# Threshold attention and a multiplicative feed-forward: scheduler-chosen order against a fixed slot order, with token-major P·V, stacked tails and paced weight loads

## Chip, cores, metric

One core of one Trainium2 chip. The metric is device time in microseconds (us) of that core; a lower time is better. Runs of one kernel spread by 1 to 3% here, so times are medians and comparisons are ratios with a 95% interval. A ratio is the mean time of one kernel's fast runs over the mean of the other's fast runs of the same rounds, so it is not quite the ratio of the medians that are quoted. The experiments ran on several chips, each beside the kernel before on the same one.

## The reference

```
scores = q @ k.T / 8                          # 8 batches x 8 heads, 576 x 576, head_dim 64
keep   = scores >= max(scores, -1) - tau
attn   = softmax(where(keep, scores, -1e9))
x      = heads_merged(attn @ v)               # 4608 tokens x 512
out    = ((x @ w1) * (x @ w2)) @ w3 @ w_out   # 512 -> 1024 -> 1024 -> 512
```

The inputs are float32. The kernel splits q and k into a bf16 high part and a bf16 low part and stacks them to a contraction of 128, so that scores are nearly exact; `w3 @ w_out` is multiplied once on the chip ("the merge"). It works on pairs of heads: 32 pairs, each with 9 units of 128 query rows (two heads x 4 blocks of 512 rows, and one unit for the two 64-row tails).

## The kernel before

The program is written as a loop over units, but without a fixed order: the scheduler chooses each engine's order by priorities. The parts that matter here (cuts marked with `...`):

```
# transposes of q and k: 64-row tails of two heads, and 4 blocks of 128 rows for each head
for hh in range(2):
    nc.tensor.transpose(tp[:, M + hh*R : M + (hh+1)*R], h[nm + "hlt"][:, h0 + hh, :, :], ident[0:64, 0:64])
    for j in range(4):
        nc.tensor.transpose(tp[:, c0:c0 + 128], hl[:, hh, j, :, :], ident[:, :])
...
PATH = "PAPAPAPAA"                       # which of two ways each unit takes
# A: copy scores to sc with their maximum (VectorE); Prelu, then Exp with row sums (ScalarE)
# P: maximum only (VectorE); e = Exp(S) (ScalarE); pm = (S >= thr) * e with row sums (VectorE): S stays in PSUM
...
# P.V, feature-major: 64 rows for each head, 512 tokens wide; the reciprocal row sums are split into bf16
# parts, transposed and spread over 128 rows by "selector" matmuls (bm, tl), copied by ScalarE, multiplied in
nc.tensor.matmul(av[o, :], lhsT=vb[:, hh, g, :], rhs=pT[:, :, g + 5*hh, :], start=(g == 0), stop=(g == 4))
...
# weights: 9 loads with a cast on the GpSimd DMA queue, issued in the first dozen units; then the merge
# at the end: feed-forward of the tail rows of batches 0-6 (448 rows), of the last batch, of the last tail
```

The softmax here doesn't subtract the row's maximum and nothing guards it: scores larger than these inputs give would overflow.

## Time and profile before

| | before |
|---|---|
| median of the first 3 runs | 653.55 us (648.12 to 661.48) |
| median in the rounds with the changed kernel | 650.84 us |
| profiled run, span | 654.1 us |
| mean granted TensorE clock | 0.927 |

Engines: PE is TensorE's matmuls, PEld its weight loads, DVE VectorE, ACT ScalarE, POOL GpSimd. These are the page's totals (busy us, share of the span, instructions) and its slices of the span in 40 parts (busy tenths; PEclk is the granted clock, DMA the mean busy share of the 16 DMA engines):

```profile
PE 536.2 (82%) x3790; PEld 286.1 (44%) x3848; DVE 444.1 (68%) x1277; ACT 390.2 (60%) x798; POOL 209.3 (32%) x463
PE   2502679789798989898998998998899998898995
PEclk9855689989999899978999999998899999998996
DMA  7999999887879678966988678977786567553101
```

PE's 82% overcounts, because the ends of pipelined matmuls overlap. PE does little in the first tenth of the span (2, 5, 0 and 2 tenths busy), where the DMA row is full. At the end DMA falls away and PE works on.

The windows of the same run (the stretch and its length, busy us and instructions of PE, PEld, DVE, ACT and POOL, then clock, DMA share and GB/s):

```profile
0.00:50.00 50.00, 12.69 (x84) 7.32 (x85) 13.60 (x46) 9.97 (x18) 27.62 (x59) 0.79 0.99 197
50.00:100.00 50.00, 29.38 (x166) 14.49 (x167) 20.37 (x61) 18.53 (x37) 11.80 (x26) 0.69 1.15 164
600.00:654.10 54.10, 46.86 (x251) 21.52 (x251) 11.72 (x24) 15.61 (x32) 0.00 (x0) 0.90 0.14 40
```

One piece of its chain of waits (start, us, what ended last):

```profile
25.50 45.50 DMA pT<-pm x2
```

In the first 100 us PE has 42 us of busy time; the chain stands 45 us on the attention's DMA transposes (pT from pm) while weights load. In the last 54 us PE runs almost alone.

The waits (engine, line, what it waited for: us in total, times, longest):

```profile
PE S L186 <- DVE pm L233: 35.3, 21, 23.7
PE S L186 <- DMA kB<-kT: 18.7, 9, 8.7
```

PE waits for score tiles in PSUM that the mask (pm) still reads, and for the copy kB of k with its halves exchanged.

### The profile page before, as it was taken

What the parts mean: (1) busy time and instruction counts of PE and PEld (TensorE: products, weight loads), DVE (VectorE), ACT (ScalarE), POOL (GpSimd) and SP (SyncE); (2) the same over time, 40 slices, a digit from 0 to 9 for tenths busy, and PEclk for the clock granted to TensorE, in tenths of its full rate; (3) what the DMA queues carried; (4) which work ended last, traced back from release to release, by engine and by line L of the source; (5) the groups of instructions that cost most, each with busy time, mean ns of one, the idle gap of its engine ahead of it and who ended that gap; (6) DMA issues with size and microseconds to landing.
All of it is one profiled execution on the core that took longest, in us unless ns stands there. A gap on an engine that the chain in (4) does not pass through costs nothing.

```text
span 654.1 us, 11488 instructions
## 1 busy us (share of the span) xinstructions
PE 536.2 (82%) x3790; PEld 286.1 (44%) x3848; DVE 444.1 (68%) x1277; ACT 390.2 (60%) x798; POOL 209.3 (32%) x463
## 2 busy tenths in 40 slices
PE   2502679789798989898998998998899998898995
PEld 1301335445354555444454454544444554453443
DVE  1602447888778787878888887885779887982221
ACT  0501356866577667856676767675667667773332
POOL 6643114442334243424343434341523331000000
PEclk9855689989999899978999999998899999998996
DMA  7999999887879678966988678977786567553101
GB/s 196 222 178 133 154 202 209 162 182 130 162 129 226 145 165 146 228 134 125 180 172 215 146 166 167 211 111 156 189 171 134 100 140 128 96 91 108 40 17 73
DMA packets 232315, 98.80 MB, mean 151 GB/s; under 512 B 198976, under 2 KB 224576, under 8 KB 231232
## 3 DMA queue, kind: packets, MB, share of 16 engines
q1 hardware_dynamic: 229040, 92.83, 70.6%
q0 software_dynamic: 3216, 5.24, 4.9%
q8 instruction: 30, 0.49, 0.4%
q14 instruction: 29, 0.24, 0.1%
HBM read 39.32 MB, written 9.44 MB: 75 GB/s over the span
## 4 chain that ended last, share of the span: by engine, by line
PE 53%; DMA 17%; DVE 13%; ACT 8%; issue 5%; POOL 2%; SPq 1%; DVEq 0%; POOLq 0%; ACTq 0%
PE ab L302 15%; PE S L186 10%; DMA pT<-pm 8%; PE yp L318 8%; PE av L281 6%; PE tp L162 5%; DMA kB<-kT 5%; DVE pm L233 3%; DVE sc L219 3%; DVE junk L229 3%; ACT y L224 3%; DMA w3t<-w_324 2%; PE tp L158 2%; PE wp L101 2%; PE tl L291 2%
## 5 line engine op out<-in xcount | busy, mean ns | idle before, releaser
L186 PE MATMUL S<-kT,qT 128*128 128x288 bf16 x512 | 140.3, 294 | 45.7 <-DVE pm L233 35.3
L224 ACT ACTIVATE y<-sc,thm 128x576 bf16<-128x576 f32 x160 | 122.8, 770 | 61.6 <-DVE thm L223 61.1
L186 PE MATMUL S<-kB,qT 128*128 128x288 bf16 x512 | 138.8, 295 | 19.0 <-DMA kB<-kT 18.7
L186 PEld LDWEIGHTS <-qT 128*128 128x128 bf16 x1024 | 94.5, 100 | 119.0 <-DMA kB<-kT 45.2
L233 DVE SCALAR_TENSOR_TENSOR pm<-S,thr,e 128x576 bf16<-128x576 f32 x128 | 103.7, 810 | 41.5 <-DMA pT<-pm 31.7
L219 DVE TENSOR_SCALAR_CACHE_REDUCE sc<-S 128x576 f32<-128x576 f32 x160 | 118.9, 748 | 15.2 <-PE S L186 11.5
L229 DVE TENSOR_SCALAR_CACHE_REDUCE junk<-S 128x576 bf16<-128x576 f32 x128 | 95.5, 746 | 31.7 <-PE S L186 31.1
L232 ACT ACTIVATE e<-S 128x576 f32<-128x576 f32 x128 | 81.9, 641 | 43.7 <-DVE junk L229 43.3
L226 ACT ACTIVATE pm<-y 128x576 bf16<-128x576 bf16 x128 | 86.9, 679 | 22.8 <-DMA pT<-pm 21.1
L307 ACT ACTIVATE ah<-ab 128x512 bf16<-128x512 f32 (+2 forms) x80 | 44.2, 553 | 75.3 <-PE ab L302 74.6
L310 DVE TENSOR_TENSOR ab<-ah,ab 128x512 bf16<-128x512 bf16 (+2 forms) x80 | 50.6, 632 | 49.1 <-PE ab L302 46.7
L318 PE MATMUL yp<-wcb,ab 128*128 128x512 bf16 (+1 forms) x276 | 72.4, 387 | 1.1 <-issue 0.2
L302 PE MATMUL ab<-xm,w2b 128*128 128x512 bf16 x245 | 67.9, 389 | 0.9 <-issue 0.2
L302 PE MATMUL ab<-xm,w1b 128*128 128x512 bf16 x232 | 66.6, 390 | 2.1 <-issue 1.5
L252 POOL CAST rhl<-rcp 128x9 bf16<-128x9 f32 x32 | 6.2, 194 | 183.8 <-DVE rcp L250 162.6
L150 POOL CAST khl<-kf 128x256 bf16<-128x256 f32 x64 | 24.0, 396 | 68.3 <-PE tp L162 68.2
L302 PEld LDWEIGHTS <-w2b 128*128 128x128 bf16 x320 | 29.5, 100 | 30.0 <-issue 9.7
L151 POOL TENSOR_TENSOR qhl<-qf,qhl 128x256 bf16<-128x256 f32 x64 | 41.9, 668 | 0.9
L151 POOL TENSOR_TENSOR khl<-kf,khl 128x256 bf16<-128x256 f32 x64 | 41.8, 667 | 0.6
L322 ACT ACTIVATE ys<-yp 128x512 f32<-128x512 f32 (+1 forms) x37 | 21.9, 592 | 31.3 <-PE yp L318 31.1
L302 PEld LDWEIGHTS <-w1b 128*128 128x128 bf16 x320 | 28.4, 101 | 27.2 <-issue 4.8
L281 PE MATMUL av<-pT,vb 128*64 128x512 bf16 x256 | 37.5, 416 | 2.6 <-DMA pT<-pm 2.0
(78 smaller groups left out, 743.7 us busy)
## 6 DMA issues: line engine op xcount, KB each, us to landing
kB<-kT SPq DMA_DIRECT2D x64, 144.0 KB, 2.9
kf<-in_k_dram SPq DMA_DIRECT2D x16, 512.0 KB, 4.5
qf<-in_q_dram SPq DMA_DIRECT2D x16, 512.0 KB, 5.2
vf<-in_v_dram SPq DMA_DIRECT2D x16, 512.0 KB, 4.4
out_dram<-ys SPq DMA_DIRECT2D x8, 1024.0 KB, 4.8
pT<-pm SPq DMA_TRANSPOSE x128, 3.5
w_324<-in_moe_w_dram POOLq DMA_DIRECT2D x4, 512.0 KB, 15.7
kt<-in_k_dram SPq DMA_DIRECT2D x16, 64.0 KB, 2.8
```

The lines of the kernel that those rows point to most:

```text
L151: nc.gpsimd.tensor_tensor(hl[:, hh, :, 1, :], src, hl[:, hh, :, 0, :], ALU.subtract)
L186: nc.tensor.matmul(sp[:, half, 0:HB], lhsT=t["qT"][:, q0:q0 + 128], rhs=kk[w][:, c0:c0 + HB], start=(w == 0), stop=(w == 1))
L219: nc.vector.tensor_scalar(sc[:, :].rearrange("p (a b) -> p a b", a=2), sp, 1.0, -3e38, ALU.mult, ALU.max, accum_out=thr[:, :])
L224: nc.scalar.activation(y[:, :], sc[:, :], AF.Prelu, scale=-1.0, bias=thm[:, :], alpha=0.125 / CUT)
L226: nc.scalar.activation(dst, y[:, :], AF.Exp, scale=-CUT, accum_out=rs)
L229: nc.vector.tensor_scalar(junk[:, :, :], sp, margin, -3e38, ALU.subtract, ALU.max, accum_out=thr[:, :])
L232: nc.scalar.activation(e[:, :, :], sp, AF.Exp, scale=0.125)
L233: nc.vector.scalar_tensor_tensor(out=dst.rearrange("p (a b) -> p a b", a=2), in0=sp, scalar=thr[:, :], in1=e[:, :, :], op0=ALU.is_ge, op1= ...
L281: nc.tensor.matmul(av[o, :], lhsT=lhsT, rhs=rhs, start=(g == 0), stop=(g == 4))
L302: nc.tensor.matmul(p[:, 0:nt], lhsT=w[:, c, f * 128:(f + 1) * 128], rhs=x(c), start=(c == 0), stop=(c == 3))
L310: nc.vector.tensor_tensor(ab[:, 0:nt], ah[:, 0:nt], ps[1][:, 0:nt], ALU.mult)
L318: nc.tensor.matmul(yp[0:c1 - c0, :], lhsT=abs_[f][:, c0:c1], rhs=wcb[:, f, :], start=(f == 0), stop=(f == NF - 1))
```

## The change

Its intent: every engine gets a fixed order in slots, one 128-row query unit a slot, with loads, casts, transposes, P·V and feed-forward placed by hand into slots; P·V becomes token-major with a column of ones in V, which gives the row sums; tails of two heads are stacked to 128 rows; weights come in 20 loads, one every second slot. The core of the diff (cuts marked):

```
-    PATH = "PAPAPAPAA"
+    PATH = "AAPAAPAAP"
+    def maximum(n, u):                     # all units: copy to SBUF with maximum, so PSUM is free at once
+        nc.vector.tensor_scalar(sc..., sp[:, :, 0:HB], 1.0, -3e38, ALU.mult, ALU.max, accum_out=mx[:, :])
+        nc.gpsimd.tensor_scalar(thr[:, :], mx[:, :], margin, None, ALU.subtract)     # was on VectorE
+    def mask(n, u): ...                    # one slot later: Prelu, Exp or (sc >= thr) * e, no accum_out
...
-            tp[:, M + hh * R:M + (hh + 1) * R] <- two 64-row transposes
+            src = hl[:, i, :, :] if i < 4 else hlt[:, hp, :, :] if i == 4 else hl[:, i - 1, :, :]
+            nc.tensor.transpose(tp[:, i * 128:(i + 1) * 128], src, ident[:, :])      # 9 of 128 rows
...
+        for un in range(10):               # P.V: 128 tokens x (64 + ones column), 5 contractions each
+            for g in range(5):
+                nc.tensor.matmul(dst, lhsT=lhsT, rhs=rhs, start=(g == 0), stop=(g == 4))   # 65 columns
+        nc.vector.reciprocal(rcp, a5[:, :, :, D])
+        nc.vector.tensor_tensor(x..., a5[:, :, :, 0:D], rcp..., ALU.mult)
+        # x is transposed back by PE and copied to xm and xt by ScalarE
-        rcp, rhl (GpSimd), rT, rTs, bm, tl, bc: the selector matmuls and their copies
...
+    with tc.manual_schedule():
+        for t in range(total + U9):
+            scores(n, u); maximum(unit t-1); evacuations; mask(unit t-2); exponent(unit t-1)
+            # casts, loads, transposes of later pairs in set slots
+            if t < 48:
+                if t % 2 == 1: next(weights, None)      # 20 loads of 512 KB
+                if t >= 30:    next(merging, None)      # the merge, slots 30 to 47
+            # P.V of the pair before in slots 4 to 7; one feed-forward step in the other slots
+            # tail rows fed forward as batches 0-3, 4-6, 7 (before: 0-6, 7)
```

## The prediction

> **What bounds it now.** No engine is full: the page shows PE 82% (pipelined, overcounted), DVE 68%, ACT 60%, POOL 32%. Three stretches count:
> - Start: in the windows, PE is busy 12.7 and 29.4 of the first two 50 us, while the DMA share is 0.99 and 1.15. The chain of waits has 45.5 us on the pT transposes from 25.5 us on: weight loads swamp the DMA engines. The attended blocks xm of the first two pairs end at 77 and 106 us.
> - Steady: from 116.5 to 584.2 us the timeline shows 28 pairs, 16.7 us each.
> - End: the last xm is at 595.5, and 58.5 us of feed-forward (FFN) follow, on PE almost alone.
>
> **Steady limit.** From starts of neighbouring matmuls in the timeline: 288 columns 123 ns, 512 columns 216 ns, 128-column transposes 56 ns. A pair's scores cost 4.6 us, transposes 1.0, FFN 24x216 = 5.2. P*V and row sums take about 2.2, the 64-row transposes about 0.7 more than full ones (132 and 151 ns around them against 56). So PE needs 13.5 of 16.7 us; the rest is waits (S waits for DVE pm 35 us and for kB 19 us in all).
>
> **What changes, per pair.**
> - PE: 50 matmuls of 65 columns replace the 10 wide ones, the selector matmuls and their transpose. The one-batch tail already has 64-column matmuls with fresh 128-column weights every 28 to 29 ns: estimate 50x30 = 1.5 us, plus 0.3 for transposing back. Stacked tails drop the drains. The Trainium skill ("TensorEngine Tiling (Array Packing)", Key Properties) says changing the tiling mode drains the engine; the 132/151 ns agree. Sum about 12.8 us, near 13.3 at the steady clock (about 0.96).
> - DVE: the copying maximum for all units, 9x0.70; three masks instead of four, from SBUF, 3x0.70; two copies 1.5; normalization 1.1; FFN 1.4: about 12.4 us. Thresholds go to POOL.
> - ACT: six two-pass units instead of five, but no 0.19 us accumulator reads: about 11.3 us. POOL about 7.
> - DMA hardly changes: 2.85 MB a pair, about 10.3 us of engine time at uncontended packet times (18 ns for 256 B).
>
> Summing each slot's larger load gives 15.6 us a pair; perfect elasticity gives 13.4. I take 14.5 (1.61 us a slot).
>
> **Sum.** First scores at about 12 us, 288 slots x 1.61 = 464; early congestion: the weights' 32 us of DMA time now spread over 40 slots beside 45 us of attention traffic, costing about 20 rather than 54; the end 36 (drain 8, last batch 96x216 = 21, small tail and store 7), because seven batches' tails move inside. Total 532 us. All on the critical path: start about 40, end about 25 (partly paid back inside), steady about 65.
>
> Predicted 532 us, 80% range 498 to 572; faster by over 2%: 0.95, within 2%: 0.03, slower: 0.02.
>
> **What would show it.** Windows: PE busy above 40 of 50 us from about 100 us on. Pair spacing about 14.5 us. Waits: no 45 us wait on pT; after the last scores about 36 us. P*V matmuls about 30 ns apart. The half-clock windows between 29 and 77 us mostly gone (skill, "TensorE: Matmul & The Clock Gate", Part 1: an idle window halves the clock; the trace's 0.5 records around the idle stretches agree).
>
> **What would make it wrong.** Fixed order turns one late transpose or threshold (POOL behind a 1.3 us subtraction) into a stall of all engines: 16 us a pair, 580. P*V at 60 ns a matmul: +45 us. Start still DMA-bound: +20. Better elasticity: 500.

## The result

| | before | changed |
|---|---|---|
| median | 650.84 us | 592.67 us (586.59 to 595.14) |
| ratio of fast runs | 1 | 0.9109 (0.8997 to 0.9222) |
| profiled span | 654.1 us | 593.4 us |

The direction was right, the size was not: 592.67 us lies 21 us above the upper end of the stated range.

A yardstick used all through: the start of the first maximum operation of each head pair on VectorE (every ninth of these 288 operations). It cuts a run into four stretches. The prediction's terms, put into the same stretches (12; five pairs of 14.5 and 20 of congestion; 26 pairs of 14.5; a last pair of 14.5 and an end of 36), add up to its 532.

| stretch (profiled runs) | before | predicted | changed | changed minus predicted |
|---|---|---|---|---|
| start to first maximum | 17.8 | 12.0 | 11.2 | -0.8 |
| pairs 0 to 4 | 120.3 | 92.5 | 117.6 | +25.1 |
| pairs 5 to 30, 26 of them | 437.9 (16.85 each) | 377.0 (14.5 each) | 399.4 (15.36 each) | +22.4 |
| pair 31 and the end | 78.1 | 50.5 | 65.2 | +14.7 |
| sum | 654.1 | 532.0 | 593.4 | +61.4 |

The page of the changed kernel, the same four lines:

```profile
PE 484.5 (82%) x4683; PEld 319.8 (54%) x4744; DVE 412.6 (70%) x923; ACT 411.3 (69%) x682; POOL 241.1 (41%) x542
PE   4447507699898789878987999998998999998895
PEclk9777857889999899989999999998999999999996
DMA  5999997996769978796979596989599978555102
```

PE still has the weak start with a full DMA row under it: only the very first slices are better than before. The windows say the same, and the last line is the stretch from the last maximum on:

```profile
0.00:50.00 50.00, 25.46 (x194) 17.62 (x195) 23.16 (x52) 21.86 (x33) 27.84 (x70) 0.78 0.95 208
50.00:100.00 50.00, 23.05 (x229) 15.97 (x230) 22.13 (x50) 21.05 (x33) 22.13 (x43) 0.71 1.07 160
550.00:593.40 43.40, 35.19 (x210) 17.22 (x213) 9.21 (x21) 12.22 (x28) 0.00 (x0) 0.89 0.11 38
```

PE was twice as busy as before in the first 50 us, and less busy in the second 50. The waits of the changed kernel that answer to those shown before:

```profile
ACT y L278 <- POOL thr L243: 38.8, 42, 8.8
PE wp L118 <- DMA w3t<-w_815: 23.9, 3, 20.3
PE S L218 <- DVE sc L240: 15.1, 19, 5.6
PE av L307 <- DMA pT<-pm: 12.7, 6, 3.9
PE av L307 <- DMA pTm<-pms_74: 8.2, 7, 2.6
```

The wait of S for the mask is gone and the one for kB nearly so (1.4 us). New, or grown from about 2 us each, are PE's waits at the merge (wp, for the DMA-transposed w3t) and at P·V (av).

**The PE part of the prediction held, as far as the trace shows it.** Taking the starts of neighbouring matmuls in the trace, and counting for each at most its columns at 2.4 GHz plus 3 ns (about the formula of the Trainium skill, "TensorE: Matmul & The Clock Gate", Back-to-back issue gap; the spacings in this trace agree, see the last section), PE's work is 12.6 to 12.8 us in three steady pairs of four and 9.5 us in the fourth, which has less feed-forward (10 to 12 matmuls of it against 26 to 28); the prediction said 12.8 on average, this is 11.9. The same count gives 11.9 us a pair for the kernel before too (pairs 8 to 19): it leaves out drains and waits, so it cannot show what the change saved on PE. Neighbouring P·V matmuls start 33 ns apart on average (median 32; predicted 30). Nothing there explains 60 us.

### The profile page after: what moved, and what is told of

Read it like the earlier page. It is cut to its first block, busy times and chain, and to the rows that moved or that the text cites. A ratio compares the mean times of both kernels' runs of the same rounds, so it can differ in the third digit from the quotient of the medians.

```text
span 593.4 us, 12945 instructions
## 1 busy us (share of the span) xinstructions
PE 484.5 (82%) x4683; PEld 319.8 (54%) x4744; DVE 412.6 (70%) x923; ACT 411.3 (69%) x682; POOL 241.1 (41%) x542
## 4 chain that ended last, share of the span: by engine, by line
PE 32%; ACT 20%; DMA 18%; DVE 13%; POOL 9%; issue 6%; SPq 2%; DVEq 0%; POOLq 0%; ACTq 0%
PE ab L360 12%; ACT y L278 8%; PE yp L375 7%; DMA pT<-pm 6%; ACT pm L280 6%; PE S L218 5%; DVE sc L240 4%; DMA pTm<-pms_74 4%; POOL khl L154 4%; POOL thr L243 2%; DMA w3t<-w_815 2%; ACT e L269 2%; DVE pm L283 2%; PE tp L191 2%; DVE ab L352 2%
## 5 line engine op out<-in xcount | busy, mean ns | idle before, releaser
L240 DVE TENSOR_SCALAR_CACHE_REDUCE sc<-S 128x576 f32<-128x576 f32 x288 | 211.5, 750 | 45.5 <-PE S L218 35.8
L243 POOL TENSOR_SCALAR thr<-mx 128x1 f32<-128x1 f32 x288 | 74.2, 258 | 284.4 <-DVE sc L240 264.6
L278 ACT ACTIVATE y<-sc,thr 128x576 bf16<-128x576 f32 x192 | 147.5, 768 | 40.3 <-POOL thr L243 38.8
L218 PE MATMUL S<-kT,qT 128*128 128x288 bf16 x512 | 143.5, 299 | 16.3 <-DVE sc L240 15.1
L280 ACT ACTIVATE pm<-y 128x576 bf16<-128x576 bf16 x192 | 131.1, 683 | 16.5 <-DMA pT<-pm 10.6
L352 DVE TENSOR_TENSOR ab<-ah,ab 128x512 bf16<-128x512 bf16 (+3 forms) x88 | 51.8, 588 | 45.1 <-PE ab L360 39.2
L283 DVE SCALAR_TENSOR_TENSOR pm<-sc,thr,e 128x576 bf16<-128x576 f32 x64 | 56.3, 880 | 36.0 <-POOL thr L243 14.4
L349 ACT ACTIVATE ah<-ab 128x512 bf16<-128x512 f32 (+3 forms) x88 | 45.1, 512 | 37.8 <-PE ab L360 37.1
L269 ACT ACTIVATE e<-sc 128x576 f32<-128x576 f32 x96 | 64.0, 667 | 0.0
L307 PEld LDWEIGHTS <-pT 128*128 128x128 bf16 x1280 | 50.3, 99 | 20.2 <-DMA pT<-pm 13.5
L360 PEld LDWEIGHTS <-w2b 128*128 128x128 bf16 x352 | 32.2, 99 | 34.3 <-issue 16.4
L118 PE MATMUL wp<-wo,w3t 128*128 128x512 bf16 x59 | 18.2, 420 | 27.1 <-DMA w3t<-w_815 23.9
L154 POOL TENSOR_TENSOR qhl<-qf,qhl 128x512 bf16<-128x512 f32 x32 | 37.0, 1157 | 8.0 <-DMA qt<-in_q_dram 5.3
```

The source lines that it names most:

```text
L154: lo.tensor_tensor(hl[1], src, hl[0], ALU.subtract)
L218: nc.tensor.matmul(sp[:, half, 0:HB], lhsT=t["qT"][:, q0:q0 + 128], rhs=kk[w][:, c0:c0 + HB], start=(w == 0), stop=(w == 1))
L240: nc.vector.tensor_scalar(sc[:, :].rearrange("p (a b) -> p a b", a=2), sp[:, :, 0:HB], 1.0, -3e38, ALU.mult, ALU.max, accum_out=mx[:, :])
L243: nc.gpsimd.tensor_scalar(thr[:, :], mx[:, :], margin, None, ALU.subtract)
L269: nc.scalar.activation(e[:, :], sc[:, :], AF.Exp, scale=0.125)
L278: nc.scalar.activation(y[:, :], sc[:, :], AF.Prelu, scale=-1.0, bias=thr[:, :], alpha=0.125 / CUT)
```

## The experiments

Each experiment has a label (e1 and so on), by which the text calls it. Starts of pairs come from single profiled runs; n is a pair's number, so that n%4 = 0 to 3 are the four pairs of a batch. The unchanged start of the kernel gave pair 5 at 128.8, 131.9 (e3) and 134.4 us (control, a slow run), so differences under about 5 us in that number are not used.

### 1. No weight bytes (e1, wrong result)

```
-            nc.gpsimd.dma_start(dst, src.rearrange("(c p) f -> p c f", p=128))
+            nc.vector.memset(dst, 0.01)
```

> Wrong result on purpose: each weight load becomes a VectorE memset of the same tile, so the attention part is unchanged but no weight bytes are moved. Theory A (the first five pairs take 117.6 us instead of five times 14.8 because the weight loads share the DMA engines with the transposes): the first maximum of pair 5 comes at 85 to 95 us instead of 128.8, total about 555. Theory B (the fixed order makes every engine wait behind the merge's matmuls, which stand at slots 30 to 47 whether or not their transposed weights have landed): the merge still stands there and still transposes by DMA, so much of the loss stays, pair 5 at 105 us or later, total 570 or more.

Measured: 565.87 us, ratio 0.8659 (0.86 to 0.8717). Pair 5 began at 103.0 us instead of 128.8, so the weights' traffic costs about 26 us. (The 20 memsets are 18 us of new VectorE work, so this may be too small.) That is between the two expectations. Pairs 3 and 4, in which the merge stands, still took 21.1 and 20.2 us against 14.8 in the steady state: 11.7 us that no weight load can explain. The merge is 64 matmuls of 512 columns, at 216 ns each 13.8 us of PE (an estimate from the spacing in the trace). **The prediction's sum has no term for it.** But it is not shown that PE's work is what it costs here: no feed-forward runs beside it before the end of pair 4 (its first matmul starts at 127.3 us in the changed kernel, 101.4 here), and PE waits for the transposed weights in these two pairs, in this run and in the changed kernel (23.9 us, above):

```profile
PE wp L118 <- DMA w3t<-w: 8.0, 3, 5.1
```

The windows of this run:

```profile
0.00:50.00 50.00, 28.54 (x230) 19.28 (x231) 35.16 (x72) 26.86 (x40) 27.98 (x71) 0.86 0.80 188
50.00:100.00 50.00, 35.42 (x354) 22.62 (x354) 38.17 (x78) 29.68 (x48) 20.52 (x41) 0.86 0.80 162
```

The DMA share falls from 1.07 to 0.80 in the second 50 us and PE has 35 us of work instead of 23.

### 2. The merge later (e2)

```
             if t < 48:
                 if t % 2 == 1:
                     next(weights, None)
-                if t >= 30:
-                    next(merging, None)
+            if 45 <= t < 63:
+                next(merging, None)
```

> Right result. Loads unchanged; the merge's steps move from slots 30 to 47 to slots 45 to 62. Theory B: the 24 us in which PE waits for w3t go, total about 570. Theory A: the wait for w3t goes, but the DMA engines have the same bytes to move in the same slots and pT waits take its place, total 583 to 593.

Measured: 595.16 us, ratio 0.9091. Pair 5 began at 106.8 us, 22 us earlier, and then pairs 5 and 6 took 29.4 and 21.4 us instead of 16.5 and 15.1: the gain was given back within two pairs. Theory B's forecast failed: the total did not fall. But this does not show that the 24 us wait for w3t cost nothing in its place, because the edit moves the merge beside the feed-forward. PE's work in pairs 5 and 6, counted as above, is 20.3 and 19.9 us here, against 14.7 and 12.6, and PE waits only 4.8 us for w3t. A part went as theory A has it: in pairs 0 to 4 PE waits 23.6 us for pT and pTm, against 11.8. By these counts the merge was paid as waiting in its old place and as PE work in the new one.

### 3. The tails split otherwise (e3)

```
-                    if n // NP in (4, B - 1):
-                        background.append(ffn_tail(*((0, 4) if n // NP == 4 else (4, B - 1))))
+                    if n // NP in (4, B - 2):
+                        background.append(ffn_tail(*((0, 4) if n // NP == 4 else (4, B - 2))))
-        background.append(ffn_tail(B - 1, B))
+        background.append(ffn_tail(B - 2, B))
```

> Right result. Tail rows are fed forward as batches 0-3, 4-5, 6-7 instead of 0-3, 4-6, 7. If the end is long because the tail of batches 4-6 falls after the last scores (541 to 558 us), which I had put inside the main phase, then about 12 to 15 us go: the end from the last maximum (52.9 us) shrinks to about 40, total about 579. Rival (the drain is limited by the last pair's transposes and P*V, not by that tail): less than 4 us.

Measured: 595.65 us, ratio 0.9096: nothing. The end from the last maximum shrank from 52.8 to 50.0 us only. Feed-forward steps are taken in order, so the tail of batches 4 and 5, now inside, pushed the feed-forward of batch 6 out into the end: its matmuls run on to 562 us in this trace. My reason (a piece of work in the wrong place) was wrong in this form. The end is a backlog of feed-forward steps; it shrinks only if steps are gained elsewhere.

### 4. P·V one slot later (e4)

```
-                if u == 4: att = attend(n - 1)
-                if u in (4, 5, 6, 7): next(att)
+                if u == 5: att = attend(n - 1)
+                if u in (5, 6, 7, 8): next(att)
     # feed-forward steps in all slots but 5 and 6 instead of 4 and 5; a batch's feed-forward starts a slot later
```

> Right result. P*V of a pair one slot later (5 to 8 instead of 4 to 7). If the 19 to 20 us pairs come from PE standing still at P*V for the pTm transpose, these fall to about 16 and the waits of av for pT and pTm (26 us) fall below 12: total about 580. Rival (the DMA engines are behind in those pairs, and whoever asks next waits): waits move to another place, total 588 to 595.

Measured: 613.16 us, ratio 0.9392: 3% slower. The waits of av for transposes did fall away, yet the slow pair stayed at 18.8 us and the others lengthened (pairs 8 to 19: 15.2, 18.8, 16.4, 14.4 for n%4 = 0 to 3, against 12.9, 19.5, 15.1, 14.8). In its window from 205 to 500 us there is a new wait:

```profile
PE xq L322 <- DVE x L314: 26.3, 18, 2.3
```

The normalization x now shares its slot with a mask on VectorE. The expectation failed, and the edit moved two things at once, so it says little about DMA. It does show how tight a hand-placed order is: this shift by one slot cost 20 us.

### 5. Thresholds back on VectorE (e5)

```
-        nc.gpsimd.tensor_scalar(thr[:, :], mx[:, :], margin, None, ALU.subtract)
+        nc.vector.tensor_scalar(thr[:, :], mx[:, :], margin, None, ALU.subtract)
```

> Right result. The threshold subtraction goes from GpSimd back to VectorE, as in the kernel before. If VectorE paces the steady state (a pair without feed-forward takes 12.87 us, one with it 14.8 to 15.1, which is about its extra VectorE work), nine ops of 0.15 us a pair add 1.0 to 1.3 us a pair: total about 620 to 630. Rival: the pace is set by ScalarE waiting for thresholds that GpSimd gives late behind its casts (38.8 us of such waits in all): total 575 to 585.

Measured: 586.26 us, ratio 0.9005 (0.8951 to 0.9058). So VectorE's throughput does not pace the steady state, though it was up to 46 or 47 us busy of 50. The four pairs n%4 = 0 to 3 took 14.8, 15.9, 15.5 and 14.9 us: the fast pair slowed and the slow pair became fast, and the sum hardly moved (61.1 against 62.2). That made me ask what fixes the sum.

### 6. No tail loads (e6, wrong result)

```
-            if hp == 1 and b + 1 < B and u in (2, 5, 8):
+            if False:            # and batch 0's casts are used again
```

> Wrong result on purpose: tail rows are loaded and cast for batch 0 only. If the tail loads, which stand in every pair n%4 = 1 right behind the pTm transpose, make that pair take 19.4 us, it falls to about 16 and the total to about 570. Rival (the backlog in the DMA engines comes from the pair before it, which has the loads of three half blocks and the 1 MB store while it runs at 12.9 us without feed-forward): the pair stays above 18 us, total above 583.

Measured: 588.06 us, ratio 0.8959 (0.8901 to 0.9016), a gain of about 1.6% by ratio whose interval overlaps that of the change. The slow pair fell from 19.5 to 17.9 us only (its profile fell in a slow run). The tail loads have a part in it, but not the main one.

### 7. The half loads in odd pairs (e8)

```
-            if n % 2 == 0 and n + 4 < NPAIR and u in (4, 6, 8):
+            if n % 2 == 1 and n + 3 < NPAIR and u in (0, 3, 6):
```

> Right result. The three 512 KB loads of a half go from even pairs (slots 4, 6, 8) to odd pairs (slots 0, 3, 6), so they leave the fast pair n%4 = 0, which also has the 1 MB store. If the DMA backlog of that pair makes the stall of the next one, pair n%4 = 1 falls from 19.4 to 16 to 17 us: total 575 to 582. Rival (the pair that starts a feed-forward is slow by its own program order): unchanged, 588 to 596.

Measured: 604.36 us, ratio 0.9277: slower. The slow pair fell to 17.4 us, as the DMA theory wants, but pair n%4 = 3 rose from 14.8 to 16.8. The stall moves with the loads; the sum of four pairs stays (62.5 us, pairs 8 to 19), but the pairs after them lengthen too. The profile is of a slow run.

### 8. Scheduler-chosen order (e7)

```
-    with tc.manual_schedule():
+    if True:
```

> Right result. The same instructions, but their order on each engine chosen by the scheduler's priorities as in the kernel before, instead of fixed as written. If the fixed order made the gain: about 630 to 660. Rival (the changed operations made it, and the order cost as much as it gave): 580 to 600.

Measured: 586.25 us, ratio 0.9002 (0.8943 to 0.9061). **With the same instructions and the scheduler's order the kernel is as fast, if not a little faster.** The gain over the kernel before does not come from the order being fixed. (The source order, which gives the priorities, is still the new one.) The slow pairs are there too: 12.7, 17.8, 15.7, 15.4 us (means of pairs 8 to 19, as above). The costliest new wait:

```profile
ACT y L278 <- POOL thr L243: 102.3, 90, 11.4
```

### 9. No half loads from the third half on (e10, wrong result)

```
-                run(load_main(n // 2 + 2, "kqv"[(u - 4) // 2]))
+                halves[n // 2 + 2, nm] = halves[n // 2, nm]      # nm = "kqv"[(u - 4) // 2]
```

> Wrong result on purpose: from the third half batch on, the 512 KB loads of q, k and v are left out and the first two halves are used again; all else is as in the changed kernel. In seven variants so far four pairs take 61 to 65 us together, however the stall is moved. If that sum is set by the DMA engines (share 0.87 to 0.94 there), it falls to 57 to 58 (12.9 + 3 x 14.8), pair n%4 = 1 from 19.4 to about 15, and with the start also relieved the total to 550 to 565. Rival (the sum is set by PE, VectorE and ScalarE in their fixed order, and the stall only makes up for the pair that ran ahead): the sum stays within 1.5 us of 62, total 582 to 592.

Measured: 567.38 us, ratio 0.8686 (0.8639 to 0.8734). The first five pairs took 103.8 us instead of 117.6, and the pairs from 5 on 14.83 us each instead of 15.36. Four neighbouring pairs (from pair 8 on), first in the changed kernel, then in this one; the last two numbers are DMA share and GB/s:

```profile
175.20:188.10 12.90, 11.27 (x133) 7.98 (x133) 11.03 (x27) 10.79 (x18) 6.19 (x13) 1.00 0.80 179
188.10:208.00 19.90, 15.71 (x144) 9.79 (x144) 13.70 (x32) 13.73 (x23) 6.89 (x17) 0.91 1.01 201
208.00:223.10 15.10, 13.60 (x142) 9.06 (x142) 13.32 (x30) 12.28 (x21) 9.26 (x20) 1.00 0.72 164
223.10:237.90 14.80, 13.77 (x145) 9.33 (x145) 11.71 (x28) 12.37 (x21) 6.39 (x14) 1.00 0.79 170
```

```profile
161.20:174.10 12.90, 11.41 (x134) 7.99 (x132) 11.03 (x27) 10.77 (x18) 6.19 (x13) 1.00 0.81 178
174.10:189.60 15.50, 14.10 (x148) 9.09 (x146) 13.73 (x33) 13.72 (x23) 7.00 (x17) 1.00 0.67 150
189.60:204.70 15.10, 13.70 (x144) 9.06 (x141) 13.32 (x31) 12.28 (x22) 9.16 (x20) 1.00 0.59 123
204.70:219.80 15.10, 13.84 (x146) 9.13 (x144) 12.59 (x28) 12.47 (x22) 6.30 (x14) 1.00 0.61 107
```

The second line of each is the slow pair. VectorE and ScalarE do the same work in it (13.7 us busy each), and PE has the same matmuls; what differs is the DMA share, 1.01 against 0.67, and 4.4 us. PE's clock differs too, 0.91 against 1.00, so a part of the 4.4 us (PE is busy for 15.7 us against 14.1) may be the lower clock that came with the waits. In the changed kernel PE stands at P·V in that pair, in the timeline (start, us, instruction, idle before and what ended it):

```profile
197.50 0.30 PE L307 MATMUL av<-vb_78,pT 128*128 128x65 bf16 x4 [1.00 <-DMA pT<-pm]
...
200.60 0.30 PE L307 MATMUL av<-vb_78,pTm 128*128 128x65 bf16 x4 [2.62 <-DMA pTm<-pms_74]
```

The pTm transpose took 4.5 us from issue to landing for that pair, against 2.7 us in an unhurried one. So the DMA engines are behind, and PE is the one that waits, because P·V comes next in its order (in the scheduler's order of e7 too, where P·V waits 18.5 us for transposes in all). This settles a part of the steady miss: 0.53 us a pair, 13.8 us over 26 pairs, and another 13.8 us in pairs 0 to 4. Taking loads away is no version to use; it says what they cost.

### 10. The score tile freed early, in the kernel before (e11)

```
-            nc.vector.tensor_scalar(junk[:, :, :], sp, margin, -3e38, ALU.subtract, ALU.max, accum_out=thr[:, :])
+            nc.vector.tensor_scalar(sc, sp, 1.0, -3e38, ALU.mult, ALU.max, accum_out=thr[:, :])
+            nc.vector.tensor_scalar(thm[:, :], thr[:, :], margin, None, ALU.subtract)
-            exp and mask read sp, thr
+            exp and mask read sc, thm      # and a fourth buffer for sc
```

> One part of the change alone, put into the kernel before: in the exp-and-mask path the maximum op also copies the scores to SBUF, and exp and mask read the copy, so that the PSUM tile of scores is free after the maximum instead of after the mask (one threshold op of 0.15 us more for each such unit). If PE's 35 us of waits for those tiles were a main part of what the steady state gained, 650 falls to 620 to 635. Rival (the gain is in the P*V rewrite and the stacked tails): 645 to 660.

Measured: 662.13 us, ratio 1.0149 (1.0098 to 1.02): 1.5% slower. The wait that this edit removes is replaced by another:

```profile
PE S L186 <- DMA kB<-kT: 46.2, 10, 33.8
```

The 35 us of waits for DVE pm, the largest of PE's in the page before, brought no gain on balance (the edit also adds 128 threshold operations of 0.15 us to VectorE): 23.7 of them are a single wait, during the weight loads of the start, and here PE waits there for DMA instead.

### 11. Scheduler order and thresholds on VectorE (e12: e5 and e7 together)

> Right result, candidate: the changed kernel with scheduler-chosen order (which had 102 us of ScalarE waits for GpSimd's thresholds) and thresholds on VectorE. If thresholds late behind GpSimd's casts cost that version time: 570 to 580. Rival (the steady sum of four pairs is conserved): 583 to 590, as for each change alone.

Measured: 582.54 us, ratio 0.891 (0.8854 to 0.8967). It was run again with five rounds beside the changed kernel on the same chip:

> The changed kernel once more, unchanged, as control on this chip: ratio to the kernel before 0.905 to 0.918.

> Scheduler order and thresholds on VectorE, once more: ratio to the kernel before 0.885 to 0.897, so 1.5 to 3% under the changed kernel. Rival (the difference was one of chips): within 1% of the control.

Measured: the changed kernel 599.25 us (587.76 to 603.33), ratio 0.9096 (0.8981 to 0.921); this version 583.28 us (580.09 to 585.98), ratio 0.8961 (0.8903 to 0.9019). The ratios' intervals overlap slightly, but each of its six runs is below each of the six of the changed kernel; several of the latter count as slow, and its two fast ones are 595.97 and 587.76. I take it as about 1.5% faster. It is the best correct version. Its pairs from 5 on take 14.87 us each, and its slow pairs are still 16 to 20 us.

### 12. Parts of the change alone, in the kernel before (e13 to e17)

Stacked tails only:

```
-            nc.sync.dma_start(y[0:64, :, :], tails)                     # q, k: 64 rows x 4 heads
+            nc.sync.dma_start(y[0:64, :, :], tails[:, 0::2, :])
+            nc.sync.dma_start(y[64:128, 0:2, :], tails[:, 1::2, :])
-                two 64-row transposes
+            nc.tensor.transpose(tp[:, M:M + 2 * R], h[nm + "hlt"][:, n % 2, :, :], ident[:, :])
```

> Right result; kernel before with the tails of q and k of two heads stacked to 128 rows, so that two 128-row transposes replace four 64-row ones in each pair. If the drains around the 64-row transposes (132 and 151 ns against 56, about 0.7 to 1.0 us a pair) lie on the critical path, the total falls by 20 to 30 us to 620 to 632. Rival (PE waits 3 us a pair anyway and only waits a little longer): within 8 us of 651.

Measured: 635.61 us, ratio 0.9761 (0.9677 to 0.9846). Pairs from 5 on: 16.24 us. A little less than expected, and well away from the rival.

Token-major P·V with the ones column only (as in the diff above, in slots 3 to 6; no accumulator reads; no selector matmuls):

> Right result; kernel before with only P*V and row sums changed: token-major with a ones column, no selector matmuls, no accumulator reads on ScalarE. If this rewrite makes the steady gain (chain of reciprocal, GpSimd split, transpose, selector matmuls, copies gone), pairs go from 16.85 to 15.5 to 16 us and the total to 615 to 630. Rival: within 8 us of 651.

Measured: 641.08 us, ratio 0.9855 (0.9759 to 0.9951), pairs 16.11 us: between the two expectations. The result was wrong by a mistake of mine: the buffers for the V tails, three for the half batches, were written again before the last reader. That changes values, not work.

Both:

> Right result; both parts. If the two make nearly all of the steady gain: pairs at 15.2 to 15.6 us, total 600 to 615. Rival (the slot arrangement, the copying maximum and the two masks fewer make it): above 630.

Measured: 631.61 us, ratio 0.9704, pairs 16.00 us, with the same mistake. Run again with four buffers:

> Right result now (four tail buffers instead of three). Ratio 0.96 to 0.98 as e15, that is about a third of what the whole change gives.

Measured: correct, 639.7 us, ratio 0.9828 (0.9745 to 0.9912), pairs 16.32 us. The two parts together give 2 to 3%, no more than the stacked tails alone within the intervals: a fifth to a third of the 8.9% of the whole change.

Paced weight loads only (20 loads, one every second unit, the merge after them):

```
-    background.append(load_weights())
-    background.append(merge_weights())
+    weights = load_weights()                    # in pieces of 512 KB
...
+        if t % 2 == 1: next(weights, None)
+        if t == 41:    background.append(merge_weights())
```

> Right result; kernel before with the weights loaded in 20 pieces of 512 KB, one every second slot, and the merge after them. The pacing as I predicted it (the attention's transposes are no longer swamped) would bring pair 5 from 138 to about 105 us and the total to about 620. If what the weights cost is DMA time that must be paid whenever they come (26 us in the changed kernel), pair 5 comes a little earlier but pairs 5 to 8 are slower, total 640 to 655.

Measured: 644.0 us, ratio 0.9884 (0.9793 to 0.9975). Pair 5 began at 120.8 us instead of 138.1, pair 8 at 178.3 instead of 191.4: 17 us won, 13 left three pairs later. Pacing does help, but by a third of the 40 us I had predicted.

## Why the prediction was wrong

**Right.** The direction, and the mechanism on PE: the drains around 64-row transposes were real (the Trainium skill, "TensorEngine Tiling (Array Packing)", Key Properties, says that a change of tiling mode drains the engine, and the spacings of 132 and 151 ns against 56 agree). Stacking the tails gained 2.4% alone (e13); it also shortens GpSimd's casts and subtractions of the tails, from 33.7 to 23.0 us in all, and the two were not told apart. The P·V matmuls start 33 ns apart (30 predicted). PE's work of 12.6 to 12.8 us in the pairs with full feed-forward was 12.8 in the sum. The first maximum came at 11.2 us (12 predicted). From 100 us on PE was busy for 42 to 46 of every 50 us, as predicted (above 40).

**The step that failed first: "early congestion: ... costing about 20 rather than 54".** Pairs 0 to 4 lost 45.1 us to five times 14.5, not 20, and of the gain of about 40 at the start only 9.3 came (pair 5 at 128.8 against 138.1). Two things were wrong in it. The weights still cost about 26 us when they are spread over 40 slots (e1), which moves the same bytes beside the same transposes. And the merge was in no term of the sum: pairs 3 and 4, where it stands, lose 11.7 us even without weight bytes. What filled the start was waiting for DMA and not PE's work: the 14.5 us hold about 5.2 us of feed-forward, which hardly runs in pairs 0 to 4, so that PE had room for the merge's 13.8 us (estimate), and it stood 23.9 us for w3t. The skill ("DMA: Bandwidth & Descriptors", Rules for kernel authors) says that DMAs from different issuing engines share the same 16 DMA engines and interleave; e1 agrees, as taking GpSimd's loads away speeds what SP issued: a pT transpose of the first 100 us took 3.6 us from issue to landing without them and 6.2 us with them (medians). About 7 us of the 45.1 (45.1 - 26 - 11.7) are left, but these costs overlap and their sum proves little: the half loads of e10 take 13.8 us of the same stretch. The prediction had named the risk ("Start still DMA-bound: +20"); the table has +25.1. The half-clock windows of the start, which it wanted mostly gone, stayed: the granted clock is 0.78 and 0.71 in the first two windows, against 0.79 and 0.69.

**The second: "DMA hardly changes".** The bytes did not change, but they now come in 9% less time. I took 10.3 us of DMA time a pair from uncontended packets and concluded that there was room; the four windows of e10's section give 13.2 us a pair in the changed kernel (share times length), and the packets of the kernel before took 13.4 us a pair (pairs 8 to 19), which could have been read beforehand. e10 shows that the half loads cost 0.53 us a pair in the steady state, 13.8 of the 22.4 us missed there. Up to pair 19, waits come in one pair of four: the pair with the least feed-forward runs ahead at 12.9 us, with the loads and the output store in it, and the next one stands for its transposes. (In pairs 20 and 21, where tail feed-forward fills the pair that ran ahead, the two take 15.8 and 15.2 us.) The other 0.33 us a pair (14.83 in e10 against 14.5) was not told apart; e5 shows only that it is not VectorE's plain throughput. The prediction's own sum of each slot's larger load was 15.6 us; 14.5 was a choice between this and 13.4, and the measured 15.36 lies near the 15.6.

**The third: "the end 36 (drain 8, last batch ... 21, small tail and store 7), because seven batches' tails move inside".** From the last maximum it was 52.8 us. The windows of the end of the changed kernel:

```profile
540.50:557.90 17.40, 14.47 (x147) 9.73 (x148) 5.44 (x14) 7.04 (x17) 0.21 (x1) 1.00 0.41 104
557.90:580.00 22.10, 21.51 (x96) 9.37 (x98) 5.50 (x8) 7.16 (x12) 0.00 (x0) 1.00 0.07 18
580.00:593.40 13.40, 7.34 (x73) 4.08 (x71) 1.78 (x8) 2.87 (x10) 0.00 (x0) 0.65 0.24 90
```

The first is the drain with the rest of batch 6 and the 192-row tail of batches 4 to 6, which is not inside the loop: 17.4 us against 8. The second is the last batch: 22.1 against 21. The third is the 64-row tail and the store: 13.4 against 7, where short matmuls wait in turn for ScalarE and VectorE (most gaps 0.27 us) and the granted clock is 0.65. e3 shows that moving the tail inside gains nothing, since another batch's work comes out instead.

**Not predicted: the order does not matter.** The prediction allowed that fixed order could stall all engines. The comparison that counts is e7: the same instructions in the scheduler's order are as fast. What fixed order buys is nothing here, and one slot's misplacement costs 3% (e4).

**What stays open.** Stacked tails, token-major P·V and pacing, each alone in the kernel before, give 2.4%, 1.5% and 1.2%, and the first two together 2 to 3%. The change gives 8.9%. The remainder lies in parts that no run separated: the earlier first unit (6.6 us), tail rows partly fed forward inside the loop (12.9 us at the end), evacuations a slot later and one mask fewer a pair. The slots' pattern of work may matter; it was only argued.

## What to carry to other kernels

Before spreading traffic out, ask whether it is late or whether it is too much: if the resource is full over the whole stretch, spreading gains little (1.2% in e16), work that is moved out of a wait may land beside other work (e2), and a speed-up elsewhere will itself fill a resource that had slack. List every piece of work once, with the place where it will be paid: the merge was in no term of my sum, and the tail that I put inside the loop was at the end. A long wait in the list (35 us for the mask) is not a gain: take it away in the old kernel first (e11); and keep the scheduler's order as a control when the order is part of the change.

## What the Trainium skill lacked or had wrong

- "TensorE: Matmul & The Clock Gate", Back-to-back issue gap: for streams of weight load and matmul it gives about 81 ns at 128 columns and about 131 ns at 512. Here such pairs start 56 ns apart at 128 columns and 216 ns at 512, and 32 ns at 65 columns (medians). Its formula for a single matmul's gap (columns / 2.4 + 2.5 ns) gives 56, 216 and 30 ns for these.
- "GPSIMD Engine Reference", Key points, says that GpSimd contends with VectorE instructions that have two SBUF inputs. That page gives no size (the skill has more on this contention elsewhere, which was not tested here). Here the mask with two SBUF inputs took 818 ns (median of 62) alone and 940 ns (median of 34, up to 1499) where a GpSimd cast or subtraction overlapped it by over 50 ns; with one input in PSUM, in the kernel before, 814 and 812 ns.
- "DMA: Bandwidth & Descriptors" has no figure for what a casting load from GpSimd costs DMA transposes beside it. Here 10.5 MB of float32 weights (32 us of the 16 engines' time by their packets in the kernel before) cost about 26 us of a run, and 256-byte packets took 104 ns on average (median 31) from 70 to 75 us, in the middle of such loads, against 24 ns on average (median 18) from 205 to 500 us.
- The same page has no figure for DMA transposes under load: issue to landing was 2.7 us for the smaller ones (pTm) when the engines had room, and 4.1 to 4.8 us in the slow pairs 9, 13 and 17, where the DMA share was 0.92 to 1.01 (but 4.5 us also in pair 11, at 0.79).
